# A second pause after the fifth step of a hand-ordered matrix product

## The chip, the cores and the metric

One core of one Trainium2 chip runs the whole program. The metric is the device time of one execution in microseconds, the median of several runs. TensorE does the matrix products, VectorE (DVE) and ScalarE (ACT) the elementwise work, SyncE (SP) issues the transfers.

## What is computed

Three layers follow each other on 4608 tokens. Only the last one matters here, but it needs the one before:

```python
attn_out = rms_norm(q @ (k.T @ v)) * g_norm     # per head
x = reshape(attn_out)                           # 4608 x 512
x = (h * clip(h + 3, 0, 6) / 6) @ w_out1        # h = x @ w_in1,  512 x 2048
x = (h * cos(h)) @ w_out2                       # h = x @ w_in2,  2048 x 512
```

Inputs and result are in fp32. The kernel splits an fp32 operand into two fp16 halves, high and low, and makes three TensorE passes for a product (high by high, high by low, low by high).

## The kernel before, in words

**Tiling.** The tokens are cut into nine blocks of 512 (`j` = 0 to 8). A block's first product of the last layer, `x @ w_in2`, is made in four groups (`gi` = 0 to 3) of 512 of the 2048 hidden columns. A group is written as a seven-product scheme (Strassen's, in Winograd's form): `group` (line 840) runs over the seven entries of `PRODS`, here n0 to n6, and each is twelve matmuls of 128x256 columns (line 862) into one of three PSUM banks, P, Q or R. P takes n0, n2, n4 and n5 one after the other and is never cleared between them. The value of P after n0, n2 and n4 is therefore copied out by ScalarE into `sn` (line 874) before the next of them may write on. VectorE adds a copy to Q or R (lines 878, 883), and the sum goes to `cos_part` (line 605), a chain of ScalarE and VectorE steps that makes h * cos(h). In it n5 reads P itself. `cos_operands` (line 635) makes the seven left operands of the second product out of four such results and `g_split` (line 624) splits each into its fp16 halves (lines 263 and 265). These go to slots in SBUF: 15 tiles of the pool `s`, two operands each, so 30 operands. A slot is free again once the second product has read the operand for the last time (line 739).

**The second product**, `(...) @ w_out2`, is the same scheme over a whole block: seven products of the block, again called n0 to n6, each cut into 16 units (`prod2`, line 726) of three matmuls of 128x256 (line 734). Its banks are called P, Q and R as well and are others than those of the first product. Here too P takes n0, n2, n4 and n5, and ScalarE copies it out after n0, n2 and n4 (line 753; the copy after n4 goes to `kv_buf`, those after n0 and n2 to `kvbd`). In this text that copy is the snapshot. The result of a step is put together and sent to memory by `evict2` (line 757). The 1 MB of right operands that a step needs is loaded by `wo_load` (line 714): two loads are ahead, and the next is issued on SP when a step has ended.

**The order on TensorE is written by the program itself**, one product of the first kind and then some units of the second, and TensorE runs it in this order. `units2` (line 773) lists the 112 units of block j - 1. They are put on the list `ready` when block j has run its n1 in group 0. The steps n0 and n1 leave their last units to the end of n1, because the operands of the last group are late. After each product of the first kind, `group` calls `pop_mm2` (line 827) with a credit of 4.2 units (RATE2, line 891); one unit costs 1, what is left is carried over up to 2, and an entry `pause` in the list sets the credit to 0, before the 1 that every entry costs is taken off:

```python
credit[0] += n
while credit[0] >= 1 and ready and can(ready[0]):
    f, *args = ready.pop(0)
    f(*args)
    credit[0] -= 1
credit[0] = min(credit[0], CAP)
```

After the last group of block 8 no product of the first kind is left, and the list is emptied alone. Generators such as `cos_part` go forward by one step at each `turn()`, twice per product. The order on ScalarE and VectorE follows the order in which the program writes their instructions; the snapshots and the copies of P have a higher priority (200 places, lines 752 and 873), the sums too (lines 761 and 877).

Of the kernel before, what the change touches and what calls it, by code (L numbers as in the profile page):

```python
# [56 lines left out]
def attention_moe_kernel(  # L57
# [715 lines left out]
    def units2(j):  # L773

        res = []
        late = []
        for n in range(7):
            for i in range(NPR):
                for mt in range(2):
                    end = i == NPR - 1 and mt == 1  # L780
                    u = (prod2, j, n, mt, i, end)
                    (late if n < 2 and i >= NPR - 2 else res).append(u)
            if n == 1:
                res += late
            if n in (1, 4):
                res.append((pause,))
        return res

    def pause():
# [357 lines left out]
    for layer in range(2):  # L1147
        for j in range(1 - layer, NSB):
            for gi in range(NG):
                hooks = {n: [] for n in range(7)}  # L1150
                last = layer == 1 and j == NSB - 1
                if layer == 0 and j == NSB - 1:
                    if gi == 0:
                        hooks[2].append(lambda: start(x2_load(0)))
                        hooks[4].append(lambda: start(x_ops(1, 0)))
                elif not last:
                    if gi == 2 and layer:
                        hooks[4].append(lambda j=j: start(x2_load(j + 1)))
                    if layer and j == 0 and gi == NG - 1:
                        hooks[6].append(lambda: free.update(raw=free["raw"] + 2))  # L1160
                    if gi == NG - 1:
                        hooks[XO].append(lambda layer=layer, j=j: start(x_ops(layer, j + 1)))
                if layer == 0:
                    if j == 1 and gi == 0:
                        hooks[1].append(lambda: start(l2_weights()))
                    if j == NSB - 1:
                        for n in range(2):
                            hooks[6].append(lambda i=2 * gi + n: fetch_i(i))
                elif gi == 0:
                    if j:  # L1170
                        hooks[LAG].append(lambda j=j: ready.extend(units2(j - 1)))
                    if j == 1:
                        hooks[0].append(lambda: [start(wo_load()) for _ in range(2)])
                seq.append((layer, j, gi, hooks))
    n = NG * (NSB - 2)
    for g in seq[:n] + [seq[n + i] for i in MIX] + seq[n + 2 * NG:]:
        group(*g)
    ready.extend(units2(NSB - 1))
    while active or ready:
        turn()  # L1180
# [31 lines left out]
```

## Time and profile before

| what | value |
|---|---|
| median of 3 runs | 1533.23 us (1532.27 to 1535.2) |
| the profiled execution, its own time | 1536.69 us |
| span of its instructions | 1534.9 us |
| TensorE busy in the span | 1499.7 us, 98% |
| VectorE busy | 1237.1 us, 81% |
| ScalarE busy | 1042.3 us, 68% |

In a timeline row "P<-xoB,wi" is a product of the first kind (line 862), "P<-wo,gs_A" are units of the second (line 734). Rows merge like instructions that follow each other, x12 is their count. The length shown for a row of matmuls goes to the modelled end of the last one (each is shown some 0.27 us long), while the next can start every 0.11 us; so the idle time in brackets is shorter than the time between the slots. "ACT kv_buf L753" as the releaser is the snapshot after n4, "ACT sn L874" the copy of P in the first product.

### The profile page before, as it was taken

What the parts mean: (1) busy time and instruction counts of PE and PEld (TensorE: products, weight loads), DVE (VectorE), ACT (ScalarE), POOL (GpSimd) and SP (SyncE); (2) the same over time, 40 slices, a digit from 0 to 9 for tenths busy, and PEclk for the clock granted to TensorE, in tenths of its full rate; (3) what the DMA queues carried; (4) which work ended last, traced back from release to release, by engine and by line L of the source; (5) the groups of instructions that cost most, each with busy time, mean ns of one, the idle gap of its engine ahead of it and who ended that gap; (6) DMA issues with size and microseconds to landing.
All of it is one profiled execution on the core that took longest, in us unless ns stands there. A gap on an engine that the chain in (4) does not pass through costs nothing.

```text
span 1534.9 us, 29088 instructions
## 1 busy us (share of the span) xinstructions
PE 1499.7 (98%) x11788; PEld 1144.5 (75%) x11788; DVE 1237.1 (81%) x2218; ACT 1042.3 (68%) x1686; POOL 3.1 (0%) x10
## 2 busy tenths in 40 slices
PE   7999999999999999999999999999999999999998
PEld 6445676766666665666666688888888888888887
DVE  4999788787978767885566799989898988989881
ACT  4676566665656645664456788888888787878771
POOL 0000000000000000000000000000000000000000
PEclk9999999999999999999999999999999999999999
DMA  7753434343434233311032133334242433333334
GB/s 214 228 164 78 129 96 125 99 131 112 127 98 125 90 92 97 127 49 56 1 104 94 66 105 143 129 120 154 95 159 92 156 111 137 124 139 120 141 118 151
DMA packets 148086, 180.16 MB, mean 117 GB/s; under 512 B 87024, under 2 KB 119792, under 8 KB 138736
## 3 DMA queue, kind: packets, MB, share of 16 engines
q1 hardware_dynamic: 147888, 178.31, 36.1%
q8 instruction: 92, 1.51, 0.4%
q14 instruction: 42, 0.34, 0.1%
q0 software_dynamic: 64, 0.00, 0.0%
HBM read 144.70 MB, written 33.55 MB: 116 GB/s over the span
## 4 chain that ended last, share of the span: by engine, by line
PE 50%; DVE 33%; ACT 13%; issue 2%; DMA 2%; SPq 1%; DVEq 0%; ACTq 0%
PE acc L681 18%; PE P L862 10%; DVE uA L614 5%; PE R L862 5%; DVE uA L619 5%; DVE gs_A L265 4%; DVE gs_S L265 4%; ACT uA L616 3%; PE h L1082 3%; PE acc L1107 3%; PE Q L862 3%; DVE c L878 2%; ACT uA L617 2%; PE po L472 2%; PE P L734 2%
## 5 line engine op out<-in xcount | busy, mean ns | idle before, releaser
L862 PEld LDWEIGHTS <-wi 128*128 128x128 f16 x5712 | 559.0, 98 | 111.6 <-issue 6.9
L681 PE MATMUL acc<-g,wo 128*128 128x512 f16 x1536 | 370.2, 380 | 2.1 <-ACT o L694 1.5
L681 PEld LDWEIGHTS <-wo 128*128 128x128 f16 x1536 | 148.9, 98 | 137.9 <-issue 4.8
L862 PE MATMUL P<-xoB,wi 128*128 128x256 f16 x1536 | 190.2, 274 | 2.5 <-ACT sn L874 2.4
L862 PE MATMUL P<-xoT,wi 128*128 128x256 f16 x1536 | 188.7, 273 | 0.5 <-ACT sn L874 0.2
L734 PEld LDWEIGHTS <-gs_A 128*128 128x128 f16 x1632 | 159.7, 98 | 20.4 <-issue 1.9
L874 ACT ACTIVATE sn<-P 128x512 f32<-128x512 f32 x204 | 119.1, 584 | 58.8 <-PE P L862 58.3
L734 PEld LDWEIGHTS <-gs_S 128*128 128x128 f16 x1392 | 136.1, 98 | 22.1 <-issue 6.4
L616 ACT ACTIVATE uA<-uA,cols 128x512 f32<-128x512 f32 x144 | 103.6, 720 | 62.6 <-DVE uA L614 61.2
L575 ACT ACTIVATE u<-c,cols 128x512 f32<-128x512 f32 x96 | 77.9, 811 | 95.0 <-DVE c L878 69.3
L734 PE MATMUL P<-wo,gs_S 128*128 128x256 f16 x888 | 114.5, 273 | 5.1 <-ACT kv_buf L753 5.1
L734 PE MATMUL P<-wo,gs_A 128*128 128x256 f16 x840 | 107.2, 273 | 1.6 <-ACT kv_buf L753 1.6
L590 DVE TENSOR_TENSOR g<-u,g 128x512 f16<-128x512 f32 x128 | 87.5, 686 | 23.3 <-ACT g L588 22.1
L577 DVE SCALAR_TENSOR_TENSOR u<-u,cols,c 128x512 f32<-128x512 f32 x96 | 71.8, 748 | 41.6 <-ACT u L575 41.3
L588 ACT ACTIVATE g<-u 128x512 f16<-128x512 f32 x128 | 80.1, 627 | 33.9 <-DVE u L577 33.4
L263 ACT ACTIVATE gs_A<-uA,cols 128x512 f16<-128x512 f32 x125 | 88.3, 713 | 16.2 <-DVE uA L619 11.3
L265 DVE SCALAR_TENSOR_TENSOR gs_A<-uA,cols,gs_A 128x512 f16<-128x512 f32 x125 | 92.6, 746 | 7.1 <-ACT gs_A L263 5.1
L612 ACT ACTIVATE uA<-c,cols 128x512 int32<-128x512 f32 x108 | 77.2, 715 | 30.0 <-DVE c L883 21.8
L862 PE MATMUL R<-xoT,wi 128*128 128x256 f16 x768 | 94.5, 273 | 0.0
L862 PE MATMUL Q<-xoB,wi 128*128 128x256 f16 x768 | 94.3, 273 | 0.0
L862 PE MATMUL R<-xoN,wi 128*128 128x256 f16 x768 | 94.3, 273 | 0.0
L619 DVE SCALAR_TENSOR_TENSOR uA<-uA,c 128x512 f32<-128x512 f32 x108 | 74.1, 686 | 23.0 <-ACT uA L617 22.1
(207 smaller groups left out, 2211.5 us busy)
## 6 DMA issues: line engine op xcount, KB each, us to landing
wo<-wod SPq DMA_DIRECT2D x63, 1024.0 KB, 4.9
ri<-in_moe_w_in_dram SPq DMA_DIRECT2D x16, 1024.0 KB, 5.9
ro<-in_moe_w_out_dram SPq DMA_DIRECT2D x16, 1024.0 KB, 5.2
x2d<-o SPq DMA_DIRECT2D x36, 256.0 KB, 2.5
xr<-x2d SPq DMA_DIRECT2D x9, 1024.0 KB, 4.8
out_dram<-o SPq DMA_DIRECT2D x36, 256.0 KB, 3.8
kv_buf<-in_k_dram SPq DMA_DIRECT2D x29, 256.0 KB, 3.2
kv_buf<-in_v_dram SPq DMA_DIRECT2D x29, 256.0 KB, 3.3
```

Of the source, the lines that this page charges most:

```text
L263: nc.scalar.activation(out=hi, in_=src, func=AF.Copy, scale=s)
L265: nc.vector.scalar_tensor_tensor(out=lo, in0=src, scalar=s, in1=hi, op0=ALU.mult, op1=ALU.subtract)
L575: nc.scalar.activation(out=u, in_=c, func=AF.Relu, scale=u0[:, gi:gi + 1], bias=b0[:, gi:gi + 1])
L588: nc.scalar.activation(out=gt[:, :, 0, sl], in_=u, func=AF.Copy)
L590: nc.vector.tensor_tensor(out=gt[:, :, 1, sl], in0=u, in1=gt[:, :, 0, sl], op=ALU.subtract)
L612: nc.scalar.activation(out=ui, in_=c, func=AF.Copy, scale=y)
L616: nc.scalar.activation(out=u, in_=u, func=AF.Sin, scale=hf)
L619: stt(out=u, in0=u, scalar=0.5 * SIG2, in1=c, op0=ALU.subtract, op1=ALU.mult)
L681: nc.tensor.matmul(out=acc[e], lhsT=w[:, a, row, e * P:(e + 1) * P], rhs=g[:, c], start=(n == 0 and i == 0), stop=(n == NF - 1 and i == 2),)
L734: nc.tensor.matmul(out=ps[:, mt], lhsT=g[:, c, pr, mt * P:(mt + 1) * P], rhs=w[:, i, a], start=(first and k == 0), stop=(end and k == 2), ...
L862: nc.tensor.matmul(out=ps[bank][:, pr], lhsT=w[:, a, A_AT[an], kk], rhs=x[:, c, kk], start=(first and pr == 0 and i == 0 and kk == 0), sto ...
L874: nc.scalar.activation(out=sn[n], in_=ps["P"], func=AF.Copy)
```

## The change

The list of units gets a second `pause` right behind the one that follows n4. The pause after n1 stays alone. Nothing else is changed.

```diff
             if n == 1:
                 res += late
             if n in (1, 4):
+                res.append((pause,))
+            if n == 4:
                 res.append((pause,))
         return res
```

## Rows read from the trace of the kernel before

**Rows 1.** The page: busy time by engine, and one line of its transfers.

```profile
PE 1499.7 (98%) x11788; PEld 1144.5 (75%) x11788; DVE 1237.1 (81%) x2218; ACT 1042.3 (68%) x1686; POOL 3.1 (0%) x10
...
wo<-wod SPq DMA_DIRECT2D x63, 1024.0 KB, 4.9
```

**Rows 2.** Busy time by stretch: blocks 6 and 8 of the last layer.

```profile
core 0: us, PE busy (x) PEld busy (x) DVE busy (x) ACT busy (x) POOL busy (x), PEclk, DMA share, GB/s
...
1270.80:1345.00 74.20, 73.54 (x675) 65.76 (x674) 66.58 (x103) 60.84 (x100) 0.00 (x0) 1.00 0.37 128
...
1419.20:1492.00 72.80, 71.88 (x660) 64.29 (x658) 60.04 (x92) 56.08 (x92) 0.00 (x0) 1.00 0.37 129
```

**Rows 3.** The waits of TensorE from 899.5 us to the end (total, times, longest).

```profile
PE P L734 <- ACT kv_buf L753: 6.7, 9, 1.0
PE P L862 <- ACT sn L874: 0.6, 1, 0.6
```

**Rows 4.** Timeline around the snapshot after n4 in block 1 (start, length).

```profile
951.59 1.15 PE L734 MATMUL P<-wo,gs_A 128*128 128x256 f16 x9
952.57 1.47 PE L862 MATMUL P<-xoB,wi 128*128 128x256 f16 x12
952.59 0.63 ACT L617 ACTIVATE uA<-uA 128x512 f32<-128x512 f32 x1
953.13 0.71 ACT L263 ACTIVATE gs_S<-uA,cols 128x512 f16<-128x512 f32 x1
953.74 0.71 ACT L612 ACTIVATE uA<-c,cols 128x512 int32<-128x512 f32 x1
954.35 0.67 ACT L753 ACTIVATE kv_buf<-P,cols 128x512 f32<-128x512 f32 x1
955.07 1.14 PE L734 MATMUL P<-wo,gs_S 128*128 128x256 f16 x9 [1.02 <-ACT kv_buf L753]
```

**Rows 5.** Timeline: the same place in block 2, and its last lines in later ones.

```profile
1027.12 1.47 PE L862 MATMUL P<-xoB,wi 128*128 128x256 f16 x12
...
1028.54 0.67 ACT L753 ACTIVATE kv_buf<-P,cols 128x512 f32<-128x512 f32 x1
...
1029.26 1.14 PE L734 MATMUL P<-wo,gs_S 128*128 128x256 f16 x9 [0.67 <-ACT kv_buf L753]
...
1400.19 1.14 PE L734 MATMUL P<-wo,gs_A 128*128 128x256 f16 x9 [0.67 <-ACT kv_buf L753]
...
1474.63 1.14 PE L734 MATMUL P<-wo,gs_A 128*128 128x256 f16 x9 [0.92 <-ACT kv_buf L753]
...
1520.11 4.09 PE L734 MATMUL P<-wo,gs_S 128*128 128x256 f16 x36 [0.78 <-ACT kv_buf L753]
```

**Rows 6.** Timeline of TensorE around the last product of the first kind.

```profile
1489.04 1.47 PE L862 MATMUL R<-xoN,wi 128*128 128x256 f16 x12
1490.35 1.47 PE L734 MATMUL R<-wo,gs_A 128*128 128x256 f16 x12
1491.66 1.47 PE L734 MATMUL R<-wo,gs_S 128*128 128x256 f16 x12
```

**Rows 7.** Timeline: n4 and its copy in block 5, groups 1 and 3.

```profile
1223.14 1.47 PE L862 MATMUL P<-xoT,wi 128*128 128x256 f16 x12
...
1224.45 0.49 PE L734 MATMUL P<-wo,gs_S 128*128 128x256 f16 x3
...
1225.05 0.58 ACT L874 ACTIVATE sn<-P 128x512 f32<-128x512 f32 x1
...
1225.76 1.04 PE L862 MATMUL P<-xoB,wi 128*128 128x256 f16 x8
...
1261.97 0.49 PE L734 MATMUL P<-wo,gs_S 128*128 128x256 f16 x3
1262.17 0.60 ACT L874 ACTIVATE sn<-P 128x512 f32<-128x512 f32 x1 [0.42 <-PE P L862]
...
1263.57 0.68 DVE L883 TENSOR_TENSOR c<-R,sn 128x512 f32<-128x512 f32 x1
```

**Rows 8.** Timeline: the one wait on a copy of P, in block 1.

```profile
909.12 1.47 PE L734 MATMUL Q<-wo,gs_A 128*128 128x256 f16 x12
...
910.53 0.57 ACT L874 ACTIVATE sn<-P 128x512 f32<-128x512 f32 x1
...
911.16 1.47 PE L862 MATMUL P<-xoB,wi 128*128 128x256 f16 x12 [0.56 <-ACT sn L874]
```

## The prediction

> **What bounds the kernel now.** I read the page first: TensorE is busy 98% of the span, the next engine, VectorE, 81% [rows 1]. The busy time by stretch then shows that the last layer, from 899.5 us on, is no exception: a block takes 74.2 us, TensorE fills 73.5, VectorE 66.6, ScalarE 60.8, all at the full clock (1.00, 2.4 GHz) [rows 2]. So only what lets TensorE stand still is worth anything, and the list of its waits has two lines: nine waits for the snapshot after n4, 6.7 us together, and one of 0.6 us for a copy of P in the first product [rows 3]. The timeline shows the mechanism. The last three units of n4 are followed by one product, and then n5 wants to write P. The snapshot starts 1.78 us after the last slot of n4 (952.57 to 954.35), because ScalarE has three other instructions in front of it, and n5 starts at 955.07, 0.05 us after the snapshot ends [rows 4]. Six later blocks do the same with a wait of about 0.67 us each, block 8 waits 0.92 and the end, where nothing stands between, 0.78 [rows 5].
>
> **What a wait really costs.** Twelve matmuls take 1.31 us from slot to slot (nine take 951.59 to 952.57, 0.98, so 0.109 each). In block 2 the product's slots end at 1027.12 + 1.31 = 1028.43 and n5 starts at 1029.26: 0.83 us lost where the row says 0.67 [rows 5]. I add 0.16 to each shown wait. Block 1 loses 1.18, blocks 2 to 7 lose 6 x 0.83 = 4.98, block 8 1.08, the end 0.94.
>
> **What the second pause does.** After the first pause the credit is -1, so the call ends; the next one has 3.2, meets the second pause, and is at -1 again. So one product of the first kind gets no units, and n5 comes one product (1.31 us) later. Nothing is added to any queue. The snapshot is done 2.09 us after n4's last slot in block 2 (1027.12 to 1029.21) and 2.45 in block 1 [rows 4, 5]; two products cover 2.62. So the waits of blocks 1 to 7 go: 1.18 + 4.98 = **6.16 us saved**. The end has no product left to put in between: nothing saved.
>
> **What it shifts.** A block has 28 products and a credit of 28 x 4.2 = 117.6. By the rule of the list it now spends just that: 112 units, 2 for pauses, and the rest lost at the pauses and in rounding; the last units of a block come right before the next block's are listed. There is no slack, so each block starts its units one product later than the block before did. In block 1 the empty place lies between the group's n0 and n1, in block 2 between n1 and n2, and so on; in block 7 it follows n6, and in block 8 it falls behind the last product. After the last product 31 units of the block before are then left instead of 4 (the 12 matmuls at 1491.66 [rows 6]). TensorE's work is the same; it only moves to the end, where TensorE is busy anyway.
>
> The empty place shortens what stands between two writes to P of the first product. The critical pair is n4 and n5: the copy is done 1.18 us after n4's last slot in group 1 and 0.80 in group 3 (1224.45 to 1225.63, 1261.97 to 1262.77) [rows 7], and TensorE may go on 0.05 later. Four units (1.31 us) normally cover it. Step by step:
> - Block 3: the shifted pause after n1 leaves three units (0.98) between n4 and n5 of group 1: 1.23 - 0.98 = 0.25 lost.
> - Block 4: two units there (0.66): 0.57 lost.
> - Block 5: the empty place is between n4 and n5 of group 3: 0.85 lost, all of it.
> - Block 6: n4 and n5 have three units, enough; n6 follows n5 directly and needs the sum from R, done 2.28 after n4 (1264.25) [rows 7]; it comes after 0.98 + 1.31 = 2.29: 0.04.
> - Block 8: n5 of the second product follows n4 with nothing in between. The snapshot then costs 2.14 with ScalarE as loaded as in block 2, against 1.08 now: 1.06 lost. With an idle ScalarE it is 0.94, as at the end [rows 5].
>
> Sum of these: 2.77. **Net 6.16 - 2.77 = 3.4 us saved.**
>
> The slowest copy of P in this layer is done 1.98 us after n4 (909.12 to 911.10 [rows 8]). With that one everywhere (1.98 + 0.05 less what stands between) blocks 3, 4 and 5 lose 1.05, 1.37 and 2.03; block 6 loses 1.05 before n5 and, its sum later by the same 1.18 as the copy, another 0.17 before n6; block 8 loses 1.42 with the snapshot of block 1: 7.1 in all, 0.9 more than is saved. With the fastest copies (0.85) blocks 3 to 6 lose 0, 0.19, 0.85 and 0.04, block 8 gains 0.14: 0.9, so 5.2 saved. I take the middle sum, since its rows are those of the very groups concerned.
>
> Other edits: the loads of right operands and the stores on SP shift with the steps that issue them; a load lands in 4.9 us [rows 1] and two are ahead of a step that lasts four products with their units, 10.5 us, so they stay hidden. The operand slots are costed at nothing, because an operand is read first about a block after it is made, and ScalarE is free 13.4 us of a block [rows 2]; if that cover goes, the second rival below is what comes.
>
> Against what: the profiled execution took 1536.69 us, of which the span is 1534.9, 3.5 above the median of the three runs. The saving is absolute, so I take it from the median: 1533.23 - 3.4 = **1529.8**.
>
> **Rivals.**
> - *All of it is kept.* The order on ScalarE is made anew, and the copies that are now wanted earlier may come earlier: in group 3 the copy started 0.20 after n4. For it: only one wait on a copy of P stands in 630 us [rows 3]. Against it: block 5 has nothing in between at all. Time: 1533.23 - 6.2 - 0.1 = 1526.9.
> - *Slots run out, and it is slower.* Holding each operand longer uses slots. Counted by the list's rule the 30 slots have 5 spare at the worst now; every block takes about one away, and from block 6 or 7 on none is left. Then a split on ScalarE (line 263) waits until TensorE has read a slot's old operand, with the copies of P behind it. If every pair n4, n5 of blocks 6 to 8 then waits as the one in rows 8 does (0.56 + 0.16), 12 x 0.72 = 8.7 are lost: 1533.23 - 3.4 + 8.7 = 1538.5. It decides from the point where no spare slot is left; against it speak VectorE's and ScalarE's free time, which grows in block 8 (60.0 and 56.1 of 72.8 us [rows 2]), and the priority of the copies. The Trainium skill says the same of the queue (PSUM — Partial Sum Buffer, section Engine vs sequencer instructions): ScalarE's queue is strictly first in, first out. The trace agrees as far as it goes: the snapshot in rows 4 had been free to run for most of its 1.78 us and stood behind three others; a copy behind a split that is itself blocked no row shows.
> - *Given back.* The order before repeats itself in blocks 2 to 7; now each block has its own. If blocks 2, 3, 4, 6 and 7 each open one more wait like rows 8, 5 x 0.72 = 3.6 go: 1533.4.
> - *It doesn't do what it says* in two of nine places (block 8, the end), as above; in the others the two pauses can't fall into one call, since the credit is -1 after the first.
>
> **Numbers.** Forecast 0.42, all kept 0.24, given back 0.17, slots 0.17. A measurement of this kernel can tell about 0.2% (3.1 us) from no change, and the forecast lies just past that. Faster: all of "all kept" and a little over half of the forecast, 0.46. Slower: nearly all of "slots" and a bit of "given back", 0.18. The rest, 0.36, is the same. The forecast alone spans 1528.0 (5.2 saved) to 1534.1 (0.9 lost). The range for all goes from "all kept" less 0.9, which is how far the lowest run lies below the median, 1526.0, to "given back" plus the 2.0 of the highest run and a part of "slots", 1536.0; it leaves out most of the 0.17.
>
> **What will show it.** Right: in blocks 1 to 7 no wait for `kv_buf` and two products between n4's last unit and n5; 31 units (93 matmuls) after the last product before the next block's begin; a wait on `sn` in block 5, group 3, of 0.7 as shown. Wrong: waits on `sn` in many groups; TensorE idle before line 862 for sums on VectorE; ScalarE idle before a split (line 263) for line 734 in blocks 6 to 8, which would be the slots; a block of 73.4 us throughout would be "all kept".

## The result, and the profile after

The changed kernel is slower: **1542.52 us**, median of six runs (1541.67 to 1543.73), against 1532.98 for the kernel before in six runs beside it (1532.11 to 1535.2). The ratio is 1.0065 [1.0055, 1.0076], so 9.5 us were lost where 3.4 were to be saved (1529.8 was forecast). Its profiled execution took 1543.69 us, the span is 1541.9.

The page of the changed kernel, busy time by engine and the load of right operands, which answer to [rows 1]. TensorE does the same 11788 matmuls; its share falls by a point, and the load takes what it took.

```profile
PE 1498.1 (97%) x11788; PEld 1141.8 (74%) x11788; DVE 1237.1 (80%) x2218; ACT 1039.6 (67%) x1686; POOL 3.1 (0%) x10
...
wo<-wod SPq DMA_DIRECT2D x63, 1024.0 KB, 4.9
```

The waits of TensorE from 899.5 us to the end (total, times, longest), changed kernel. All line numbers from 787 on are two higher than before: line 864 is the first product, line 876 the copy of P.

```profile
PE P L864 <- ACT sn L876: 10.5, 12, 1.7
PE P L734 <- ACT kv_buf L753: 4.7, 5, 1.7
```

Against [rows 3] the two lines have changed places. The snapshot costs 4.7 instead of 6.7, the copy of P 10.5 instead of 0.6. That is most of the result: a wait for one copy out of PSUM has become a larger wait for the other one.

The timeline of the changed kernel in block 2, where [rows 5] had 0.67 shown. Two products now stand between the last units of n4 and the first of n5, and the wait is gone:

```profile
1025.77 0.82 PE L734 MATMUL P<-wo,gs_A 128*128 128x256 f16 x6
...
1026.42 1.47 PE L864 MATMUL Q<-xoB,wi 128*128 128x256 f16 x12
...
1027.73 1.47 PE L864 MATMUL P<-xoT,wi 128*128 128x256 f16 x12
1027.81 0.68 ACT L753 ACTIVATE kv_buf<-P,cols 128x512 f32<-128x512 f32 x1
...
1029.05 1.15 PE L734 MATMUL P<-wo,gs_S 128*128 128x256 f16 x9
```

And the last product of the first kind with what follows it, answering to [rows 6] and to the last lines of [rows 5]. n5 of block 8 now follows n4 with nothing in between, as predicted:

```profile
1485.33 1.47 PE L864 MATMUL R<-xoN,wi 128*128 128x256 f16 x12
1486.64 1.15 PE L734 MATMUL P<-wo,gs_S 128*128 128x256 f16 x9
1489.50 4.09 PE L734 MATMUL P<-wo,gs_A 128*128 128x256 f16 x36 [1.71 <-ACT kv_buf L753]
```

**Where the new waits stand.** Some 5 us later, in group 3 of the same block 2, this is what TensorE and ScalarE do between n4 and n5 of the first product:

```profile
1032.65 1.47 PE L864 MATMUL P<-xoT,wi 128*128 128x256 f16 x12
1033.15 0.71 ACT L263 ACTIVATE gs_S<-uA,cols 128x512 f16<-128x512 f32 x1
...
1033.76 0.62 ACT L617 ACTIVATE uA<-uA 128x512 f32<-128x512 f32 x1
...
1033.96 1.47 PE L734 MATMUL P<-wo,gs_S 128*128 128x256 f16 x12
1034.28 0.71 ACT L263 ACTIVATE xoT<-tb,cols 128x512 f16<-128x512 f32 x1
...
1034.89 0.71 ACT L263 ACTIVATE xoT<-ta,cols 128x512 f16<-128x512 f32 x1
...
1035.51 0.71 ACT L263 ACTIVATE gs_A<-uA,cols 128x512 f16<-128x512 f32 x1
1036.12 0.58 ACT L876 ACTIVATE sn<-P 128x512 f32<-128x512 f32 x1
...
1036.75 1.47 PE L864 MATMUL P<-xoB,wi 128*128 128x256 f16 x12 [1.32 <-ACT sn L876]
```

n4's slots end at 1033.96. The copy of P starts 2.16 us later, behind four instructions that ScalarE does without a pause. Four units (1.31) stand between n4 and n5, as in the kernel before, but they no longer cover it: 1.48 us are lost from slot to slot. In the kernel before, the copy in group 3 starts 0.20 after n4, and ScalarE has been idle for 0.42 just before [rows 7]. The same wait stands in group 3 of blocks 1 to 4 (1.53, 1.48, 1.45, 1.86), and smaller ones in others.

The busy time by group says why it is this group. First the kernel before, groups 0 to 3 of block 5 (us, then busy time and count by engine):

```profile
core 0: us, PE busy (x) PEld busy (x) DVE busy (x) ACT busy (x) POOL busy (x), PEclk, DMA share, GB/s
1194.00:1212.70 18.70, 18.70 (x174) 16.77 (x172) 16.31 (x26) 14.33 (x24) 0.00 (x0) 1.00 0.36 128
1212.70:1230.70 18.00, 18.00 (x168) 16.13 (x166) 15.60 (x24) 14.46 (x24) 0.00 (x0) 1.00 0.36 132
1230.70:1249.67 18.97, 18.97 (x176) 17.00 (x174) 16.17 (x26) 14.75 (x25) 0.00 (x0) 1.00 0.32 112
1249.67:1268.90 19.23, 18.55 (x171) 16.48 (x169) 19.20 (x31) 18.00 (x31) 0.00 (x0) 1.00 0.41 137
```

Then the changed kernel, the four groups of block 2:

```profile
968.36:987.02 18.66, 18.66 (x173) 16.74 (x171) 16.50 (x27) 14.16 (x24) 0.00 (x0) 1.00 0.45 152
987.02:1005.14 18.12, 17.85 (x165) 15.85 (x163) 15.57 (x25) 14.50 (x25) 0.00 (x0) 1.00 0.36 132
1005.14:1024.13 18.99, 18.99 (x176) 17.02 (x174) 16.27 (x25) 15.11 (x25) 0.00 (x0) 1.00 0.33 112
1024.13:1042.32 18.19, 16.87 (x156) 14.96 (x154) 18.12 (x30) 16.33 (x28) 0.00 (x0) 1.00 0.23 77
```

Group 3 carries work that the others don't: `x_ops` (line 525) makes the operands from the next block's `x` there (below also called the right operands of the first product, since `x` is the right-hand argument of its matmuls). These are seven splits on ScalarE and VectorE and four sums on VectorE. VectorE is busy 19.20 of 19.23 us in it, ScalarE 18.00. TensorE had a pause of its own in that group, the 0.83 of the snapshot. The second pause takes units out of group 3 (28 in blocks 2 to 7 before, 22 to 24 after: the empty place itself, and the credit that is lost at it) and puts them into other groups and behind the last product. TensorE's own part of the group falls from 18.3 us to 16.7, the elementwise part stays, and TensorE comes to P too early.

**All of it in one table.** "Lost" is the time between matmuls of lines 734 and 862 (the lines of the kernel before) beyond the 0.109 us from slot to slot, in us, summed over blocks 1 to 8 by the group it stands in; "tail" is what is lost after the last product. The units are those placed in groups 0 to 3 of block 4. The last columns are the median and the ratio to the kernel before in the same set of runs.

| kernel | units | lost g0 | g1 | g2 | g3 | tail | sum | us | ratio |
|---|---|---|---|---|---|---|---|---|---|
| before | 29 27 28 28 | 0.7 | 0.2 | 0 | 7.2 | 0.9 | 9.1 | 1532.98 | |
| after | 30 26 29 23 | 3.4 | 2.4 | 0.3 | 9.9 | 2.8 | 18.8 | 1542.52 | 1.0065 [1.0055, 1.0076] |
| p1_twice | 30 22 29 27 | 6.3 | 2.9 | 0.4 | 12.2 | 2.1 | 23.9 | 1548.6 | 1.0108 [1.0091, 1.0125] |
| rate_all_44 | 31 29 27 25 | 1.0 | 1.1 | 0.6 | 15.6 | 0.9 | 19.3 | 1544.32 | 1.0078 [1.0063, 1.0094] |
| rate_g0_48 | 34 26 24 28 | 0.9 | 10.2 | 0 | 8.1 | 0.9 | 20.1 | 1543.19 | 1.0073 [1.0058, 1.0088] |
| rate_g3_5 | 29 26 28 29 | 2.9 | 2.7 | 0 | 0 | 0.9 | 6.5 | 1529.98 | 0.9983 [0.9974, 0.9992] |
| g3_5_again | 29 26 28 29 | 2.9 | 2.7 | 0 | 0 | 0.9 | 6.6 | 1529.77 | 0.9983 [0.9975, 0.9992] |
| two_g3_48 | 30 27 28 27 | 11.5 | 0.2 | 0 | 0 | 0.9 | 12.6 | 1537.56 | 1.0026 [1.0015, 1.0037] |
| two_g3_54 | 28 25 28 31 | 3.4 | 5.2 | 0 | 0 | 0.9 | 9.5 | 1532.52 | 0.9999 [0.9989, 1.0009] |
| one_g3_46 | 28 25 28 31 | 0.7 | 0.2 | 0 | 6.0 | 0.9 | 7.8 | 1531.91 | 0.9993 [0.9983, 1.0003] |
| n45_g3_5 | 29 26 28 29 | 4.8 | 3.9 | 0 | 4.9 | 0.9 | 14.5 | 1537.49 | 1.0032 [1.0020, 1.0045] |
| hold_after | 30 26 29 23 | 8.2 | 2.6 | 0 | 6.9 | 2.8 | 20.5 | 1545.11 | 1.0076 [1.0061, 1.0091] |
| hold_before | 29 27 28 28 | 3.2 | 3.7 | 0 | 4.0 | 0.9 | 11.9 | 1536.69 | 1.0022 [1.0013, 1.0032] |
| x_once_after | 30 26 29 23 | 0.7 | 0.6 | 0 | 4.4 | 2.8 | 8.6 | 1533.39 | 1.0002 [0.9992, 1.0012] |
| x_once_before | 29 27 28 28 | 0.7 | 0.2 | 0 | 5.1 | 0.9 | 7.0 | 1532.12 | 0.9990 [0.9980, 1.0000] |
| x_no_dve_after | 30 26 29 23 | 0.7 | 0.4 | 0 | 8.0 | 2.8 | 11.9 | 1535.74 | 1.0016 [1.0005, 1.0027] |
| x_no_act_after | 30 26 29 23 | 3.6 | 2.7 | 0 | 7.7 | 2.8 | 16.9 | 1540.07 | 1.0047 [1.0034, 1.0061] |
| pool_after | 30 26 29 23 | 6.7 | 3.2 | 0.3 | 14.4 | 2.8 | 27.5 | 1551.8 | 1.0117 [1.0095, 1.0139] |

In hold_before, x_no_dve_after and one_g3_46 one execution each was far longer than the rest (4049.7, 4049.43 and 1564.66 us); the ratios leave it out, the medians don't.

The changed kernel loses 9.8 us more than the kernel before by this count (18.82 - 9.07), and its median is 9.5 longer: the waits are the whole of it.

### The profile page after: what moved, and what is told of

The parts are those of the page before. It is cut to its first block, busy times and chain, and to the rows that moved or that the text cites. A ratio compares the mean times of both kernels' runs of the same rounds, so it can differ in the third digit from the quotient of the medians.

```text
span 1541.9 us, 29110 instructions
## 1 busy us (share of the span) xinstructions
PE 1498.1 (97%) x11788; PEld 1141.8 (74%) x11788; DVE 1237.1 (80%) x2218; ACT 1039.6 (67%) x1686; POOL 3.1 (0%) x10
## 4 chain that ended last, share of the span: by engine, by line
PE 59%; DVE 23%; ACT 10%; DMA 3%; SPq 3%; issue 2%; DVEq 0%; ACTq 0%
PE acc L681 17%; PE P L864 13%; PE R L864 6%; PE P L734 5%; PE Q L864 3%; DVE uA L619 3%; DVE uA L614 3%; DVE gs_A L265 3%; PE R L734 3%; PE h L1084 3%; PE acc L1109 3%; DVE gs_S L265 3%; SPq L438 2%; ACT uA L616 2%; DVE c L880 2%
## 5 line engine op out<-in xcount | busy, mean ns | idle before, releaser
L864 PEld LDWEIGHTS <-wi 128*128 128x128 f16 x5712 | 558.8, 98 | 123.7 <-issue 18.8
L734 PEld LDWEIGHTS <-gs_S 128*128 128x128 f16 x1380 | 135.1, 98 | 15.6
L734 PE MATMUL P<-wo,gs_A 128*128 128x256 f16 x876 | 112.6, 273 | 4.7 <-ACT kv_buf L753 4.7
L734 PE MATMUL P<-wo,gs_S 128*128 128x256 f16 x852 | 108.4, 273 | 0.0
L614 DVE SCALAR_TENSOR_TENSOR uA<-uA,cols,c 128x512 f32<-128x512 int32 x108 | 80.6, 746 | 14.9 <-ACT uA L612 14.0
L265 DVE SCALAR_TENSOR_TENSOR gs_A<-uA,cols,gs_A 128x512 f16<-128x512 f32 x117 | 86.2, 746 | 6.0 <-ACT gs_A L263 5.7
L617 ACT ACTIVATE uA<-uA 128x512 f32<-128x512 f32 x144 | 89.5, 622 | 1.5
```

Source lines behind the costliest of these rows:

```text
L265: nc.vector.scalar_tensor_tensor(out=lo, in0=src, scalar=s, in1=hi, op0=ALU.mult, op1=ALU.subtract)
L614: stt(out=u, in0=ui, scalar=nk, in1=c, op0=ALU.mult, op1=ALU.add)
L617: nc.scalar.activation(out=u, in_=u, func=AF.Square, scale=SIG2 ** 0.5)
L734: nc.tensor.matmul(out=ps[:, mt], lhsT=g[:, c, pr, mt * P:(mt + 1) * P], rhs=w[:, i, a], start=(first and k == 0), stop=(end and k == 2), ...
L864: nc.tensor.matmul(out=ps[bank][:, pr], lhsT=w[:, a, A_AT[an], kk], rhs=x[:, c, kk], start=(first and pr == 0 and i == 0 and kk == 0), sto ...
```

## The experiments

Three theories were tried against each other. **V**: group 3 is full on VectorE and nearly so on ScalarE, and units taken out of it come back as waits. **D**: the shift of the units from block to block costs, by the short gaps or the slots. **S**: only the place of the copies of P in ScalarE's order is bad. Each diff is against the changed kernel unless it says otherwise.

### Where the pause stands, and where the units go

**p1_twice** moves the second pause to the step n1.

```diff
-            if n == 4:
+            if n == 1:
                 res.append((pause,))
```

> The added pause stands behind the one after n1 instead of the one after n4. Credit lost per block, the shift by one product per block and the 30-odd units left at the end are those of the changed kernel; but the empty place lies in group 1 or 2, and group 3 keeps 27 or 28 units instead of 22 to 24. Theory V (VectorE has no idle time in group 3, where the next block's operands are split too; TensorE time taken out of that group comes back as waits for copies of P): the waits on sn in group 3 of 1.5 us and more are gone, the old waits for the snapshot (0.83 us a block) stay, 1532 to 1536 us. Rival D (the shift from block to block, with the operand slots it uses up, is what costs): 1540 to 1544 us as the changed kernel.

It took 1548.6 us, worse than either theory said. Group 3 has 27 units again, but the pauses now meet other copies: TensorE waits 12.0 us in nine places for the snapshot after n4, and the copies cost 3.8. A part is of another kind. After three of these waits, of 2.33, 2.12 and 2.01 us, the granted clock of TensorE is 0.50 (1.2 GHz) for some 3 us, and 47 matmuls start every 0.21 us instead of 0.109: 4.9 of the 23.9 us in the table. No such stretch stands in the last layer of the changed kernel, whose longest wait is 1.71. The stretch after the wait of 2.33 (p1_twice, the clock is the third number from the end):

```profile
1109.10:1112.40 3.30, 3.30 (x18) 2.32 (x17) 3.30 (x6) 2.23 (x5) 0.00 (x0) 0.50 0.25 84
```

So a second pause is dear at either place, and V's figure was wrong here, also without these 4.9 us.

**rate_all_44** has two pauses and enough credit that a block spends all of its units: nothing shifts.

```diff
-RATE2 = 4.2
+RATE2 = 4.4
```

> The changed kernel with a credit of 4.4 per product instead of 4.2 in all groups: no shift from block to block, always 5 slots to spare, the empty place always after n0 of group 3, and 25 units in group 3 against 28 before and 22 to 24 changed. Theory V: group 3 still has too little TensorE work beside VectorE's 19 us; each block waits 1 to 1.5 us on sn there and saves 0.83 at the snapshot, 1533 to 1538 us. Rival D: the shift is gone, the saving of 6.2 us remains, 1526 to 1528 us.

Every block from 3 to 7 is the same, the tail is 0.9 as before, no operand is held longer from block to block, and yet 2.0 us a block are lost in group 3 (25 units), 1.77 of them at the copy before n5. It is as slow as the change. So neither the shift nor the slots are needed for such a loss, and **D falls** as its main cause; x_once_after, below, keeps the shift and loses little. What the shift does cost in the changed kernel is 0.8 us at the tail.

**rate_g3_5** keeps both pauses and gives group 3 back its units; **rate_g0_48** gives group 0 a higher credit instead. Both end the shift.

```diff
-            pop_mm2((RATE2 if j else RATE1) if layer else 16.0 / 7.0)
+            pop_mm2(((5.0 if gi == 3 else RATE2) if j else RATE1) if layer else 16.0 / 7.0)
```

```diff
+            pop_mm2(((4.8 if gi == 0 else RATE2) if j else RATE1) if layer else 16.0 / 7.0)
```

> The changed kernel with a credit of 5.0 per product in group 3 alone: no shift, 5 slots to spare, two products between the snapshot and n5 as in the changed kernel, and 29 units in group 3. Theory V: group 3 has 18.66 us of TensorE work without waits, VectorE needs 19.1 to 19.2; the snapshot's wait is gone, some of it comes back on sn or is carried into the next group: 1527 to 1531 us, and no wait on sn over 0.6 us in group 3. Rival D: 1526 to 1528 us. If it stays at 1540 or more both fall, and the order on ScalarE made with two pauses is to blame.

> The changed kernel with a credit of 4.8 per product in group 0 alone: no shift, 5 slots to spare; n4 of the second product ends one product earlier, so that the empty place lies after n6 of group 2, where VectorE is idle 2.8 us, and group 3 keeps 28 units (34, 26, 24 and 28 by group). Theory V: the waits for the snapshot go without waits on sn in group 3, 1526 to 1530 us. Rival D: the same, 1526 to 1528 us.

With 29 units in group 3 the kernel is **faster than before**: 1529.98 us, 0.9983 [0.9974, 0.9992]. The waits of TensorE from 899.5 us on in rate_g3_5 show what the change was meant to give: one snapshot is left, the one at the end.

```profile
PE P L864 <- ACT sn L876: 2.1, 9, 0.6
PE P L734 <- ACT kv_buf L753: 0.8, 1, 0.8
```

Its timeline between n4 and n5 in group 3 of block 2:

```profile
1029.40 0.71 ACT L263 ACTIVATE xoT<-tb,cols 128x512 f16<-128x512 f32 x1
...
1030.01 0.71 ACT L263 ACTIVATE xoT<-ta,cols 128x512 f16<-128x512 f32 x1
...
1030.20 1.47 PE L864 MATMUL P<-xoT,wi 128*128 128x256 f16 x12
...
1030.62 0.71 ACT L263 ACTIVATE gs_S<-uA,cols 128x512 f16<-128x512 f32 x1
...
1031.23 0.71 ACT L263 ACTIVATE gs_A<-uA,cols 128x512 f16<-128x512 f32 x1
...
1031.85 0.58 ACT L876 ACTIVATE sn<-P 128x512 f32<-128x512 f32 x1
...
1033.15 0.60 PE L864 MATMUL P<-xoB,wi 128*128 128x256 f16 x4
```

ScalarE has the same kinds of instructions in front of the copy, `xoT` and `xoT` and then splits of the second product's operands, at the same 0.61 us each. What is different is TensorE: it reaches the end of n4 (1031.51) when ScalarE is one split from the copy, where the changed kernel got there four instructions too soon.

rate_g0_48 is against V as it was put. Group 3 has its 28 units and loses 1.11 all the same, and group 1, where VectorE has time, loses 1.33 (1.11 at n5, 0.22 before n2). So the count of units in group 3 alone doesn't decide; where the units before and after it stand seems to count too, but no run shows how.

**two_g3_48** and **two_g3_54** vary the credit of group 3 with two pauses (4.8 and 5.4 in place of 5.0); **one_g3_46** is the kernel before with one pause and 4.6 in group 3; **g3_5_again** is rate_g3_5 once more.

> Two pauses, a credit of 4.8 in group 3: no shift, the empty place after n0 of group 3, and 27 units in group 3 (25 with 4.4 everywhere, 29 with 5.0, where 2.0 and 0.0 us were lost in group 3). Theory V (VectorE's 19.1 us of work in group 3 must be matched by TensorE work): 7 products and 27 units are 18.0 us, so about 1.0 us is lost a block in group 3, against 0.83 before: 1532 to 1537 us. Rival P (what counts is only that the second pause stands before n5, and the rate of 5.0 was lucky): as with 5.0, 1528 to 1531 us.

> Two pauses, 5.4 in group 3: 31 units there, 28, 25 and 28 in the others. Theory V: 19.3 us of TensorE work in group 3, more than VectorE needs, nothing lost there; the other groups have 0.5 to 1 us less and may lose a little on sn; 1527 to 1531 us.

> One pause as in the kernel before, with 4.6 in group 3: 31 units there, 28, 25 and 28 in the others, n4 ending at the same place. It parts the rate from the pause. Theory V: the snapshot still has one product before n5, so its 0.8 us a block stay while group 3 loses nothing else: 1531 to 1535 us, some 4 us behind the same distribution with two pauses. Rival R (the rate alone made the run with 5.0 faster, the pause adds nothing): 1528 to 1531 us.

> Two pauses and 5.0 in group 3 once more, beside the next kernel: 1528 to 1531 us, a ratio of 0.997 to 0.9995.

With 4.8, group 3 is without waits but ends after 18.01 us, all of which VectorE is busy, and what it didn't finish is late in the next group: 1.46 us at n5 of group 0 in every block from 3 on. With 5.4 the other groups become short, 0.71 in group 1, and the 1532.52 us lie above V's 1527 to 1531. In between, at 5.0, 0.63 a block is left. One pause with 31 units in group 3 gains too little to tell (0.9993 [0.9983, 1.0003]): its snapshot still costs 0.65 a block. But it stands against the forecast that it would be some 4 us behind two pauses with the same units: that kernel is two_g3_54, and it took 1532.52 us against 1531.91. At equal units the second pause gained nothing; what it saved at the snapshot came back as copies in groups 0 and 1. The gain of 2.3 us belongs to the spread that two pauses and 5.0 give together, and one pause with the spread of rate_g3_5 was not run. The repeat gave 1529.77 us, 0.9983 [0.9975, 0.9992].

**n45_g3_5** was to take the last 0.6 a block too, by moving one unit of each group from behind n5 to between n4 and n5.

```diff
+            pop_mm2(((5.0 if gi == 3 else RATE2) + {4: 1.0, 5: -1.0}.get(n, 0.0) if j else RATE1) if layer else 16.0 / 7.0)
```

> The same, with one unit more of credit after n4 and one less after n5, so that five or six units instead of four or five stand between n4 and n5, the pair that still waits 0.20, 0.36 and 0.07 us a block on the copy of P. Theory V: group 3 keeps its units and these waits go, up to 7 x 0.6 = 4.4 us: 1525.5 to 1529 us. If the order made for ScalarE shifts with it and the waits turn up elsewhere: 1529 to 1534 us.

It lost instead: 1537.49 us. The waits on copies are many and short (4.6 us in 15 places), but a snapshot wait of 0.58 is back in group 3 of every block. The order of the elementwise work follows the order of the program, so moving single units moves all of it.

### Is it the order on ScalarE alone?

**hold_after** and **hold_before** put each split behind the last copy of P written before it, in the changed kernel and in the one before.

```diff
+                    made = nc.scalar.activation(out=sn[n], in_=ps["P"], func=AF.Copy)
+                if layer:
+                    last_copy[:] = [getattr(made, "ins", made)]
...
+            with tc.issue_after(last_copy[0]):
+                nc.scalar.activation(out=hi, in_=src, func=AF.Copy, scale=s)
```

> The changed kernel, but each split of the last layer is held on ScalarE behind the last copy of P (sn) that the program had written before it; no instruction is added or taken away. In block 2, group 3, twelve instructions then stand on ScalarE between the copies of n0 and n4 instead of fifteen. Theory S (the copy of n4 is late because ScalarE's order has splits in front of it that were ready early): 3 x 0.61 = 1.8 us earlier in each block's group 3, the waits on sn of 1.5 us go, 1530 to 1536 us. Theory V (VectorE has no time left in group 3, whatever the order): the splits that are held come late for VectorE and what follows, the time comes back as other waits, 1540 to 1544 us.

> The same hold in the kernel before, where no split or one stands between the end of n4 and its copy in group 3. Theory S: little to win or lose on sn, and the snapshot's 0.83 us a block stays unless it too moves forward, 1528 to 1534 us. Theory V: the same or slower, 1532 to 1538 us.

The waits in group 3 fall from 9.9 to 6.9 us and those in group 0 rise from 3.4 to 8.2: 1545.11 us. In the kernel before the same edit costs 3.3 us. Work that is put behind the copy is late for what comes after. **S alone falls.**

### The extra work of group 3, taken away

These leave work out, from block 2 on: **x_once** takes the operands of block 1 for all later blocks, so the splits and sums of `x_ops` are not made (in the changed kernel and in the one before). **x_no_dve_after** keeps ScalarE's high halves and leaves out VectorE's low halves and sums; **x_no_act_after** keeps VectorE's part and leaves out the high halves.

```diff
+        if layer and j >= 2:
+            xops[layer, j] = xops[layer, j - 1]
+            free["raw"] += 1
+            return
```

```diff
...
+            if layer and j >= 2:
+                nc.scalar.activation(out=t[:, 0], in_=src, func=AF.Copy, scale=s)
...
```

```diff
...
+            if layer and j >= 2:
...
+                nc.vector.scalar_tensor_tensor(
+                    out=t[:, 1], in0=src, scalar=s, in1=src, op0=ALU.mult, op1=ALU.subtract
+                )
...
```

> The changed kernel with the splits and sums of the first product's right operands left out for blocks 2 to 8 (seven splits on ScalarE, seven and four sums on VectorE a block, all in group 3; block 1's operands are used again). The shift from block to block, the slots and the units at the end are those of the changed kernel. Theories S and V (group 3 has too much elementwise work for its TensorE time): the waits in group 3 go, 1526 to 1533 us. Rival D (the shift and the slots): 1538 to 1543 us.

> The kernel before with the same splits and sums left out for blocks 2 to 8. Theories S and V: the snapshot still has only one product in front of n5, so 0.2 to 0.8 us a block stay; 1527 to 1532 us, and the changed kernel without these splits is at most 3 us slower, or faster. Rival D: the changed kernel stays some 9 us slower than this one.

> The changed kernel; of the operands of the first product for blocks 2 to 8 ScalarE still makes the seven high halves a block, but VectorE's seven low halves and four sums are left out (block 1's low halves stay in use). Theory V (VectorE is the engine that has no time left in group 3): most of the 9.5 us comes back, 1532 to 1536 us, as with both parts left out (1533.4). Rival A (ScalarE is the one: its seven splits stand in front of the copies of P): 1538 to 1543 us.

> The other half: VectorE still makes the low halves and the sums of blocks 2 to 8, ScalarE's seven high halves are left out (block 1's stay in use). Theory V: VectorE is as full as in the changed kernel, 1538 to 1543 us. Rival A: 1532 to 1536 us. If both halves alone bring back about half, both engines are at their limit.

Without that work the change costs 1533.39 - 1532.12 = 1.3 us instead of 9.5; leaving it out takes no matmul away. (1533.39 lies just above the 1526 to 1533 of S and V, since 4.4 us of waits in group 3 stay.) **So the next block's operands are what makes the second pause dear.** The halves show how. Without VectorE's part the waits outside group 3 are gone but for 0.9 us in block 1, which the kernel before loses too, and 0.2 in block 4 (6.1 to 1.1), but 8.0 us in group 3 stay. Its window in block 2, which answers to the last row of the changed kernel's above:

```profile
1022.67:1040.55 17.88, 16.87 (x156) 14.95 (x154) 15.02 (x24) 16.93 (x30) 0.00 (x0) 1.00 0.25 79
```

VectorE now has 2.9 us free, and TensorE still waits 1.17 there, because two splits `xoT` and another stand ahead of the copy on ScalarE (timeline of x_no_dve_after):

```profile
1032.50 1.47 PE L742 MATMUL P<-wo,gs_S 128*128 128x256 f16 x12
1032.51 1.33 ACT L561 ACTIVATE xoT<-xr,cols 128x512 f16<-128x512 f32 x2
...
1033.73 0.72 ACT L263 ACTIVATE gs_A<-uA,cols 128x512 f16<-128x512 f32 x1
1034.35 0.58 ACT L884 ACTIVATE sn<-P 128x512 f32<-128x512 f32 x1
...
1034.98 0.71 PE L872 MATMUL P<-xoB,wi 128*128 128x256 f16 x5 [1.01 <-ACT sn L884]
```

Without ScalarE's part it is the other way: 7.7 us in group 3 and 6.4 outside it, as much as in the changed kernel (6.1). VectorE's part is worth 6.9 of the 18.8 us of waits, ScalarE's 2.0, both together 10.2. So V is half of the truth. VectorE's full group delays the groups after it. In group 3 itself either part alone is enough to keep most of the loss: 8.0 us with ScalarE's splits alone, where VectorE has 2.9 us free, 7.7 with VectorE's part alone, 9.9 with both and 4.4 with neither. The 4.4 stand almost all in blocks 3 to 5, and the operands don't explain them.

How a late VectorE reaches a copy is seen in the changed kernel in block 7, group 0, before the wait of 0.96:

```profile
1352.07 0.69 DVE L619 SCALAR_TENSOR_TENSOR uA<-uA,c 128x512 f32<-128x512 f32 x1
...
1352.23 1.47 PE L734 MATMUL R<-wo,gs_A 128*128 128x256 f16 x12
1352.79 0.72 ACT L263 ACTIVATE gs_A<-uA,cols 128x512 f16<-128x512 f32 x1 [0.78 <-DVE uA L619]
1353.42 0.71 ACT L263 ACTIVATE gs_A<-us,cols 128x512 f16<-128x512 f32 x1
...
1354.03 0.57 ACT L876 ACTIVATE sn<-P 128x512 f32<-128x512 f32 x1
...
1354.65 0.60 PE L864 MATMUL P<-xoB,wi 128*128 128x256 f16 x4 [0.96 <-ACT sn L876]
```

ScalarE stands idle for 0.78 us before a split whose input VectorE hasn't finished. The last matmul of n4 had its slot by 1352.23; the second split begins 1.2 us later, and the copy still comes after it. The Trainium skill says so of the queue (PSUM — Partial Sum Buffer, section Engine vs sequencer instructions): ScalarE's queue is strictly first in, first out; the row agrees, with the blocked split that no row of the kernel before had shown.

**pool_after** moves the four sums of `x_ops` to GpSimd for blocks 2 to 8 (the expectation counts five; there are four in a block).

```diff
-        tt = nc.vector.tensor_tensor
+        tt = nc.gpsimd.tensor_tensor if layer and j > 1 else nc.vector.tensor_tensor
```

> The changed kernel with the five sums of the first product's right operands of blocks 2 to 8 made on GpSimd instead of VectorE (lines 549 to 554): VectorE has 4 x 0.69 = 2.7 us a block less to do in group 3, TensorE and ScalarE the same. Theory V: of the 9.5 us lost a good part comes back, 1534 to 1539 us, if GpSimd is fast enough that no split waits for it. If ScalarE's own work in group 3 is what is too much, it stays at 1541 to 1544 us.

It tells nothing on V: at 1551.8 us it is slower, because the sums became the new lateness. ScalarE waits 10.6 us in seven places for a sum before a split, and a sum takes twice as long as on VectorE (see the last section).

## Why the prediction was wrong

**Right.** The credit's arithmetic held: nothing was added to any queue, the empty place walks by one product a block (in group 3, behind n0 at 949.80 in block 1, behind n1 at 1026.42 in block 2, behind n6 at 1412.29 in block 7), and 147 units follow the last product instead of 120. 112 of them are block 8's own, so 35 are left of the block before instead of 8: 27 more, as the 31 for 4 of the prediction said, which was four short at both ends. The tail cost 1.87 + 0.94 where it had been 1.08 + 0.94: 0.8 lost, 1.06 predicted. In blocks 1, 2, 4 and 6 the snapshot waits are gone as told (0.05 us is left in block 4).

**The first wrong step: "The critical pair is n4 and n5: the copy is done 1.18 us after n4's last slot in group 1 and 0.80 in group 3."** These came from [rows 7] and were kept as constants while the change took 1.6 us of TensorE's work out of the group they belong to. The lateness of a copy isn't the copy's own; in these traces it is how far ScalarE is behind TensorE at that point. In group 3 of block 2 the copy went from 0.80 to 2.74 us after n4 (2.16 and 0.58 long). Predicted for the copies (with the sum in block 6) were 1.71 us (0.25 + 0.57 + 0.85 + 0.04); they cost 12.4 beyond what block 1 had already lost before. The bound from the slowest copy in [rows 8], 1.98 everywhere, gave nothing for group 3 of blocks 1 to 4, since it too only looked at the pairs that the empty place shortens. Those four places alone lost 6.3.

**The reason behind it: [rows 2] was read by the block.** VectorE at 66.6 of 74.2 us and ScalarE with 13.4 us free looked like cover. By group, VectorE has 0.03 us free in group 3 and 2.4 to 2.8 in each of the others; ScalarE 1.2 there and 3.5 to 4.4 elsewhere. The cover was in the wrong groups. One more row of the same view would have shown it, and with it that the snapshot's 0.83 us fell into the one group whose elementwise work had no time to spare.

**The second: "So the waits of blocks 1 to 7 go: 1.18 + 4.98 = 6.16 us saved."** 3.46 were: 1.12 are lost in block 3, 0.91 in block 5, 0.67 early in block 8. Two products cover a snapshot that is done 2.09 after n4's last slot, not one that waits in the same queue as the late copies. In block 5 there is another reason. The part on the kernel before says that TensorE runs the order that the program writes; here it doesn't quite. The three units that the program writes behind n5 should have left n4 and n5 next to each other; two of them come ahead of n5 in the trace, so that the snapshot has one product to hide behind, as in the kernel before, and n5 lost 0.44 where 0.85 was predicted. What moved them no run shows.

Together: 3.46 saved on snapshots, less 12.4 on copies and sums, less 0.8 at the tail, is 9.7 lost, and 9.5 were measured.

**The rivals.** *Slots run out* forecast 1538.5, the nearest in time, but the time was lost for another reason: waits of 1.5 us stand already in block 1, where the slots had not run out, and rate_all_44, without a shift, loses as much. Its picture of a copy behind a blocked split was right, its cause wasn't; what blocks the split in the row above is VectorE. The slots do run out, as it said: in blocks 7 and 8 ScalarE stands idle before a split until line 734 has read a slot's old operand, in five places, 2.7 us together. Neither the kernel before nor rate_all_44 has such a wait.

```profile
ACT gs_S L263 <- PE Q L734: 1.3, 3, 0.5
ACT gs_S L263 <- PE P L734: 0.8, 1, 0.8
ACT gs_S L263 <- PE R L734: 0.6, 1, 0.6
```

The first of them stands at 1373.19, and the last wait of TensorE for a copy of P at 1354.65, so they delayed no copy of P that TensorE waits for. Before the two snapshots that TensorE still waits for after them (at 1415.58 and 1489.50), ScalarE has been idle again. *Given back* named the right thing, each block opening waits like [rows 8], but with 0.72 in five blocks against the 12.4. *All kept* stood on the hope that the new order would bring the copies earlier; it brought them later in group 3, and in some blocks in the others too. Of what was to show the prediction wrong, the first item came, waits on `sn` in many groups, and the third, the slots.

**What stays open.** How a given spread of units turns into waits isn't explained to the single copy. p1_twice, rate_g0_48 and n45_g3_5 all came out slower than the load by group suggests, with waits where VectorE had time (in group 1 of block 4 of rate_g0_48 it is busy 14.98 of 19.01 us). The order on ScalarE and VectorE is made anew for each of them, and the length of ScalarE's row ahead of a copy (none to four instructions) can't be read from the credits.

## What to carry to other kernels

Read the load of the engines by the stage whose timing the change touches, and not over a period that repeats: an engine at 90% of a block can be at 100% of the quarter that matters. A wait of TensorE in a stage where another engine is full may be that engine's time and not waste; here taking it out saved only where about as much TensorE work was put back into the same stage, and not at every such spread. Two pauses with a credit of 5.0 in group 3 took 1529.98 us (0.9983 [0.9974, 0.9992]; 2.3 us less, the best version that was run); with 4.8 they lost 5, with 5.4 they changed nothing, and without more credit they cost 9.5.

## What the runs showed of the hardware

GpSimd's sums in pool_after against VectorE's in the changed kernel, groups of instructions by line from 1000 to 1400 us (busy us, mean ns | idle before); spans on GpSimd are rough. First pool_after:

```profile
L265 DVE SCALAR_TENSOR_TENSOR gs_S<-uA,cols,gs_S 128x512 f16<-128x512 f32 x62 | 48.8, 794 | 8.6 <-ACT gs_S L263 8.0
...
L550 POOL TENSOR_TENSOR tb<-ta,xr 128x512 f32<-128x512 f32 x6 | 9.0, 1502 | 0.5
```

Then the changed kernel:

```profile
L265 DVE SCALAR_TENSOR_TENSOR gs_S<-uA,cols,gs_S 128x512 f16<-128x512 f32 x62 | 45.7, 746 | 7.8 <-ACT gs_S L263 7.3
...
L550 DVE TENSOR_TENSOR tb<-ta,xr 128x512 f32<-128x512 f32 x6 | 4.1, 685 | 0.0
```

The same sum of 128x512 in fp32 takes 1502 ns on GpSimd and 685 on VectorE, 2.2 times as long. The Trainium skill states about twice for an operation with two inputs (GPSIMD Engine Reference, section 4.1, Engine selection); the rows agree. VectorE's splits in these rows became 48 ns longer on average (746 to 794), and not evenly. Of the splits of 128x512 on line 265 between 1000 and 1400 us of pool_after, the 16 that overlap a sum on GpSimd took 1160 ns on average (740 to 1766), the 166 that overlap none 748.
